# Key weights in two row pieces, five tiles only centred, two turned tiles copied by VectorE

## The chip, the cores and the metric

The kernel runs on one core of one Trainium2 chip. A core has TensorE (matrix products, in PSUM), VectorE, ScalarE, GpSimd and SyncE, which issues most of the DMAs; each works through its own queue of instructions in order, and they wait for each other through semaphores. In the profile they are PE (with PEld for its weight loads), DVE, ACT, POOL and SP. The metric is the device time of one execution in microseconds (us); the time of a kernel is the median of its runs.

## What is computed

One transformer block, forward and backward. The sequence has 2048 rows of 640, in bf16. The first half is linear attention with 32 heads of 20; the second a gated MLP of width 1728. The outputs are the block's output and the gradients of x and of the five weights.

```python
h  = x + A_ref(layernorm(x), wqkv, wo)
h2 = h + B_ref(layernorm(h), w1, w3, w2)

def A_ref(x, wqkv, wo):                        # per head
    q, k, v = split(x @ wqkv)
    phi = lambda t: where(t > 0, t + 1, exp(t)) + 1e-6
    pq, pk = phi(q), phi(k)
    kv  = einsum("bhsd,bhse->bhde", pk, v)
    z   = einsum("bhsd->bhd", pk)
    num = einsum("bhqd,bhde->bhqe", pq, kv)
    den = einsum("bhqd,bhd->bhq", pq, z) + 1e-6
    return (num / den) @ wo

out, vjp = jax.vjp(f, x, wqkv, wo, w1, w3, w2)
return out, *vjp(grad_out)
```

The layer norm subtracts each row's mean and divides by its standard deviation. Two facts about it matter here. A factor that belongs to a row can be applied after a product with that row instead of before. And `exp` and `relu` on ScalarE take such a factor (`scale`) at no extra instruction.

## The kernel before

The order of the work is written out by hand (a manual schedule): the program text fixes the order of every engine's queue, and pools of tiles with a fixed number of buffers fix what waits for what. The 2048 rows are 16 tiles of 128 rows, called tile 0 to tile 15 (t).

**Phase 1** is the loop over t near line 540, and takes the first 50 us. For each tile it needs the row statistics, the normalised rows turned so that the 640 columns lie on the partitions (`pqT`), the key features `pk_all`, and for some tiles the query features.

- *Statistics* (`Stats.part`, lines 145 to 155, `stat` in the step lists, "S"): two BN_STATS, an aggregate and an add on VectorE, then a power of -1/2 on GpSimd, which gives the factor `rs`.
- *Normalising* (`p1_norm`, line 247, "N", "A" and "L"): subtract the mean and multiply by `rs`, on VectorE; for the tiles 10, 12 and 14 on ScalarE (`on_act`), with a bias `nb` that GpSimd makes (line 170). In the step list "N" and "A"/"L" say when it is emitted: "N" before the tile's own features, "A" behind them, "L" last.
- *Turning*: tiles 0 to 7 on TensorE (`p1_tr`, line 253: five transposes into a PSUM tile `tr`, then one ScalarE copy to `pqT`, line 260); tiles 8 to 15 by a DMA transpose (line 251) that `p1_norm` issues on SP.
- *Key features*: `p1_mm` (line 274) multiplies two halves of 320 columns into a PSUM tile `big`, of which there are two; `phi` (line 290) takes `exp` and `relu` of it on ScalarE into `mq` and `rq` (three buffers each); a held closure `rest`, "R" in the step lists, does the minimum and the add on VectorE (lines 299, 300). The turn of tile t+1 stands between the two halves of tile t.
- *Query features*: in the steps 6, 7, 9 and 11, `q_tile` does the same with tiles 0 to 3. It uses the same two `big` tiles, the same `mq` and `rq`, and the same ScalarE queue.
- In the steps 3 to 6 `ghh_chunk` puts five matmuls of 512 columns of another product behind each tile. From step 7 on `m_part` (line 430) multiplies key features with the rows.

Tile 0 is only centred (`RAW = 1`): it is turned without its factor, `exp` and `relu` apply `rs`, and `p1_scale` (line 264, "C") multiplies the rows on VectorE in step 3, since `m_part` and the store of the normalised rows need them whole. Its key features come in two halves with four ScalarE instructions (line 535), each behind its own piece of the key weights.

`v_steps` lists, for each step t, what VectorE does and in which order.

**SP's queue at the start** is x row 0, x row 1, key weights columns 0 to 319, x row 2, key weights columns 320 to 639, x row 3, x rows 4 and 5, then transposed loads (`w2T`, `g2T`), x rows 6 to 9, `w2T`, the query weights in one piece, x rows 10 to 15. ("Row" stands for 128 rows.)

**Later places that the change touches.** Behind phase 1 the residual rows are loaded again (`load_x(0, 6)`), for the attention output (`f2_at`, lines 655 to 664), whose weights `Wp` come by five DMA transposes (line 709). Behind the second backward stage `q_parts` (line 1219) issues five DMA transposes `tri` (line 1226), read by the product `gkvT` (line 1388); SP also issues there the transposed normalised rows `load_xnT` (line 1242), the transposed query weights `load_wqT` (line 1299) and the key features `load_pk` (line 1410). The last loop (line 1335) computes 35 blocks of the gradients of w1 and w3; the first seven store each block in two halves.

Of the kernel before, what the change touches and what calls it, by code (L numbers as in the profile page):

```python
# [55 lines left out]
def kernel(  # L56
# [74 lines left out]
    class Stats:  # L131
# [10 lines left out]
                for j in range(2):  # L142
                    self.part(src, t, j)

        def part(self, src, t, j, mid=None):
            if j == 0:
                self.st[t] = cp.tile([P, 2, 6], F32, name="st6", bufs=4)
            V.bn_stats(out=self.st[t][:, j, :], in_=src[:, t, j * HD:(j + 1) * HD])
            if j == 0:
                return  # L150
            V.bn_aggr(out=self.mv[:, t, :], in_=self.st.pop(t)[:])
            if mid is not None:
                mid()
            V.tensor_scalar(out=self.ve[:, t:t + 1], in0=self.mv[:, t, 1:2], scalar1=EPS_LN, scalar2=None, op0=ALU.add)
            G.tensor_tensor(out=self.rs[:, t:t + 1], in0=self.ve[:, t:t + 1], in1=mhalf[:, 0:1], op=ALU.pow)
# [27 lines left out]
    def load_wq(a, b):  # L183
        dma(out=wqkv[:, :, a * HD:b * HD], in_=wq_v[:, :, a * HD:b * HD])

    def load_x(a, b):
        dma(out=x_sb[:, a:b, :], in_=xS[:, a:b, :])

    load_x(1, 2)
    A.activation(sg[:], zero[:], AF.Exp)  # L190
    load_wq(2, 3)
    load_x(2, 3)
    load_wq(3, 4)
    load_x(3, 4)
    load_x(4, 6)

    mask = cp.tile([P, DT, M_MAX], BF16, name="mask")

# [40 lines left out]

    XT_DMA = 8  # L240
    WARM = 34
    RAW = 1

    def on_act(t):
        return t > XT_DMA and t % 2 == 0
# [1 line left out]
    def p1_norm(t):  # L247
        xn = x_sb[:, t, :]
        (ln1.norm_act if on_act(t) else ln1.norm)(xn, xn, t)
        if t >= XT_DMA:  # L250
            dmaT(out=pqT[:, :, t * P:(t + 1) * P], in_=xn)

    def p1_tr(t, parts=((0, DT),)):
        xn = x_sb[:, t, :]
        for a, b in parts:
            tr = ps.tile([P, DT, P], BF16, name="tr", bufs=2)
            for c in range(a, b):
                T.transpose(tr[:, c, :], xn[:, c * P:(c + 1) * P], ident[:])

            A.copy(out=pqT[:, a:b, t * P:(t + 1) * P], in_=tr[:, a:b, :])  # L260

    def p1_scale(t):
        xn = x_sb[:, t, :]
        V.tensor_scalar(out=xn, in0=xn, scalar1=ln1.rs[:, t:t + 1], scalar2=None, op0=ALU.mult)

    def p1_half(acc, t, n0):
        for c in range(DT):
            T.matmul(acc, lhsT=pqT[:, c, t * P:(t + 1) * P], rhs=wqkv[:, c, n0:n0 + HD], start=(c == 0),  # L268
                     stop=(c == DT - 1))

    def p1_acc():
        return ps.tile([P, 2, 512], F32, name="big", bufs=2)

    def p1_mm(t, n0, between=None, halves=None):
        acc = p1_acc() if halves is None else None
        for j in range(2):
            p1_half(acc[:, j, 0:HD] if halves is None else halves[j][:, 0:HD], t, n0 + j * HD)
            if j == 0 and between is not None:
                between()
        return acc  # L280

    def two(ap):
        return ap.rearrange("p (j n) -> p j n", j=2)
# [3 lines left out]
    def phi_tiles():  # L287
        return [p1.tile([P, D], BF16, name=n, bufs=3) for n in ("mq", "rq")]

    def phi(acc, dst, t, parts=None):  # L290

        mq, rq = parts or phi_tiles()
        if parts is None:
            kw = dict(scale=ln1.rs[:, t:t + 1]) if t < RAW else {}
            A.activation(two(mq[:]), acc[:, :, 0:HD], AF.Exp, **kw)
            A.activation(two(rq[:]), acc[:, :, 0:HD], AF.Relu, **kw)

        def rest():
            V.tensor_scalar(out=mq[:], in0=mq[:], scalar1=1.0, scalar2=1e-6, op0=ALU.min, op1=ALU.add)
            V.tensor_tensor(out=dst, in0=mq[:], in1=rq[:], op=ALU.add)  # L300
        held.append(rest)
# [157 lines left out]
    zero_pads()  # L459
    load_w2T(0, 2 * P)  # L460
    load_g2T(0)
    load_x(6, 10)
    load_w2T(2 * P, 4 * P)
    load_wq(0, 2)
    load_x(10, ST)
    def warm_up(n, warm):
        for _ in range(n):
            T.matmul(warm[:, 0:P], lhsT=ones[:], rhs=ones[:], start=True, stop=True, skip_group_check=True)
# [12 lines left out]
    def stat(t):  # L481
        ln1.run(x_sb, t, t + 1)
        if on_act(t):
            ln1.bias(t)
# [1 line left out]
    ln1.part(x_sb, 0, 0)  # L486
    ln1.part(x_sb, 0, 1, center_first)
    p1_tr(0, ((0, 2), (2, DT)))
    warm_up(8, p1_acc()[:, 0])
    stat(1)  # L490
    p1_norm(1)
    ln1.part(x_sb, 2, 0)
    ln1.part(x_sb, 2, 1)
    ln1.part(x_sb, 3, 0)
    p1_norm(2)
    ln1.part(x_sb, 3, 1)
    ln1.part(x_sb, 4, 0)
    p1_norm(3)
    ln1.part(x_sb, 4, 1)
    w13 = [go for c0, c1 in ((0, 2), (2, 4), (4, 5)) for go in load_w13(c0, c1)]  # L500
    w13 += [lambda: dma(out=w1[:, :, F:FP], in_=rows(B_w3)[:, :, F - FL:F])]

    def load_wo():
# [2 lines left out]
    trickle = {4: w13[0], 5: lambda: w13[1](0, 1), 6: lambda: w13[1](1, 2), 12: w13[2]}  # L506

    R = None
    v_steps = {1: (R, ("N", 4)), 2: (("S", 5), R, ("N", 5)), 3: (("S", 6), R, ("N", 6), ("C", 0)),
               4: (("S", 7), R, ("N", 7), ("S", 8)), 5: (R, ("N", 8), ("S", 9)), 6: (R, ("N", 9), ("S", 10)),  # L510
               7: (("S", 11), R, R, ("A", 10), ("L", 11)), 8: (("S", 12), R, R, ("S", 13)),
               9: (("N", 13), R, ("S", 14), ("B", 12)), 10: (R, R, ("S", 15)), 11: (R, ("A", 14), ("L", 15))}
    V_OPS = {"S": stat, "N": p1_norm, "C": p1_scale}

    def xn_out(g, q):
        sl = slice(g * TPC, (g + 1) * TPC)
# [9 lines left out]
    M0 = {7: (0, 1, 2), 8: (3, 4, 5)}  # L526
    M0.update({t: (t - 3,) for t in range(9, ST)})
    for t in range(ST):
        first = None
        if t < RAW:  # L530
            first = phi_tiles()
            kh = [ps.tile([P, 512], F32, name="k0", tag="m", bufs=2) for _ in range(2)]

            def act(i, j):
                A.activation(first[i][:, j * HD:(j + 1) * HD], kh[j][:, 0:HD], (AF.Exp, AF.Relu)[i],
                             scale=ln1.rs[:, t:t + 1])

            def between():
                act(0, 0)
                p1_tr(t + 1)  # L540
                act(1, 0)
            k = p1_mm(t, D, between, kh)
            act(0, 1)
            act(1, 1)
        else:
            k = p1_mm(t, D, (lambda: p1_tr(t + 1)) if t + 1 < XT_DMA else None)
        steps = v_steps.get(t, (R,) * len(held))
        for step in steps:
            if step is R:
                held.pop(0)()  # L550
            elif step[0] in V_OPS:
                V_OPS[step[0]](step[1])
        phi(k, pk_all[:, t, :], t, first)
        for when in ("A", "B", "L"):
            for step in steps:
                if step is not R and step[0] == when:
                    p1_norm(step[1])
            if when == "A" and t in QT:
                q_tile(QT.index(t))
        if 3 <= t < 7:  # L560
            ghh_chunk(t - 3, lambda: ps.tile([P, 512], F32, name="gp", tag="m", bufs=2))
        m_part(0, M0.get(t, ()))
        if t >= 11:
            V.memset(bd[:, t - 11, :], 0.0)
            make_mask(t - 11)
        if t >= 9:
            m_part(1, [2 * (t - 9), 2 * (t - 9) + 1])
        for f, *n in outs.get(t, ()):
            f(*n)
        if t in trickle:  # L570
            trickle[t]()
# [66 lines left out]
        m_part(4, range(11, ST), (j,))  # L638
        m_end(4, (j,))
    ps.release()  # L640
    load_x(0, 6)


    ps = pool("pap", space=PSUM)
# [299 lines left out]
    def kv3():  # L944
# [2 lines left out]

    run((q_late, 10, f2_mT), (q_late, 11, kv3), (phi_rest,),
        (q_late, 12, lambda: (f2_wT(0), f2_wT(1))), (q_late, 13, lambda: (f2_wT(2), f2_wT(3))),
        (f2_wT, 4), (phi_rest,), (q_late, 14), (r_T, 4), (r_head, 5), (r_prod, 7),  # L950
        (q_out, 10, 14), (mlp_ghh, 4),
        (q_late, 15), (w2_room,), (sig_table,), (f2_half, 0, 0), (f2_half, 1, 0), (f2_half, 2, 0), (f2_half, 3, 0), (mlp_ghh, 5),
        (f2_half, 0, 1), (r_store, 4, 5), (f2_half, 1, 1), (f2_hn, 0), (r_store, 5, 6), (f2_half, 2, 1), (f2_hn, 1),
# [358 lines left out]
    load_xnT(1)  # L1312
    part(4)
    part(4)
    load_xnT(2)
    part(20)
    V.reduce_sum(out=gz[:], in_=gz8[:], axis=AX.X)


# [58 lines left out]
        for _ in range(n):  # L1378
            next(jobs, None)

    load_xnT(3)
    load_wqT(0)
    fill(4)
    for m, (a, b) in enumerate(M_H):
        n = (b - a) * DH
# [14 lines left out]
    small = bv.tile([P, ST, D], BF16, name="small", tag="hnN")  # L1400
    mN, gkv_b, gm = (small[:, n:n + DT] for n in (0, DT, 2 * DT))
    gzd = small[:, 3 * DT, :].rearrange("p (m q) -> p m q", q=P)
    dma(out=mN, in_=m_v)
    dma(out=rows(dwoT_d), in_=dwoT[:])

    dx = pool("dx", "right")

    def load_pk(c):
# [2 lines left out]

    gzb = dx.tile([P, D], F32, name="gzb")
    g_k = gqkv[1] = U1.tile([P, ST, D], BF16, name="g_k", tag="S0")
    for n in range(4):
        load_pk(n)

    for i, (c, ms) in enumerate(SQ_BLOCKS):
        unload(square(wqT[:, 2 * DT:, :], gkvT, i), gm[:, i, :])
# [136 lines left out]
    for i, (f0, f1) in enumerate(blocks):  # L1555
        n = f1 - f0
        for m in range(DT):
            last = (i, m) == (len(blocks) - 1, DT - 1)
            for a, b in ((0, n - P), (n - P, n)) if last else ((0, n),):
                c = (a + b) // 2  # L1560
                halves = ((a, c), (c, b)) if i * DT + m < 7 else ((a, b),)
                out = [(x + y - a, z + y - a, to) for y, w in halves for x, z, to in both_grads(m, f0 + y, f0 + w)]
                grad_job(hnN, m, lambda t: gb[i][:, t, a:b], b - a, out, A.dma_start)
        load_block(i + 2)
        if 0 < i <= 4:
            gw2_out(i - 1)
        if i < 4:
            gw2_turn(i)
# [36 lines left out]
```

## Time and profile before

| What | Value |
|---|---|
| median of 3 runs | 820.98 us (819.28 to 821.57) |
| the profiled execution | 820.36 us, its span 818.6 us |
| granted TensorE clock | 1.00 |
| PE busy | 811.6 us (99% of the span) |
| DVE, ACT, POOL busy | 452.7, 324.8, 131.7 us |
| DVE busy between 10 and 35 us | 22.36 of 25 us |
| ACT busy between 10 and 35 us | 22.52 of 25 us |
| first matmul of key features | 6.61 us from the span's start |
| from 700 us on | PE alone, DVE under 3 us in all |

The span goes from the first to the last instruction; 1.76 us of the profiled execution's time lie around it. The page gives the busy time of an engine with what each group of instructions cost, the time that it stood idle before them, and what ended that. Matmuls overlap, so PE's busy share hides waits shorter than a matmul; a wait is better seen in the timeline, from start to start. A line of the timeline is: start, duration, engine, line of the program, operation, written tile <- read tiles, shapes, how many were merged, and in brackets the idle time and what ended it. In a merged line the duration goes from the first start to the last end.

### The profile page before, as it was taken

The numbers are of one execution on the slowest core, as the hardware profiler recorded it, in microseconds if no ns is written. First come the engines' busy times: TensorE is split into PE (matmuls) and PEld (weight loads), VectorE is DVE, ScalarE is ACT, GpSimd is POOL, SyncE is SP. The second block draws the span as 40 slices with busy tenths as digits, with TensorE's granted clock in tenths as the row PEclk, the third lists the DMA queues.
The fourth block names the chain that finished last, engine by engine and source line by source line (L and its number), as shares of the span: only waits on it lengthen the run. The fifth ranks groups of instructions, "written<-read, shape, count | busy, mean of one in ns | idle before, by whom it ended". The sixth has DMA issues, their size and how long they took to land.

```text
span 818.6 us, 13711 instructions
## 1 busy us (share of the span) xinstructions
PE 811.6 (99%) x5261; PEld 501.6 (61%) x5292; DVE 452.7 (55%) x973; ACT 324.8 (40%) x609; POOL 131.7 (16%) x198
## 2 busy tenths in 40 slices
PE   9999999999999999999999999999999999999998
PEld 6777544555555555754577777777777777544444
DVE  7859997998898566300057777772781544200000
ACT  7856688665565666011112212222212334211111
POOL 2243333323222212100001111110220000000000
PEclk9999999999999999999999999999999999999999
DMA  9899899696485556999877877269994888979991
GB/s 262 207 242 277 206 276 302 207 244 174 128 209 158 169 168 168 239 254 243 233 178 181 218 194 193 58 111 181 269 217 93 179 193 153 249 175 235 221 239 37
DMA packets 335889, 162.46 MB, mean 198 GB/s; under 512 B 252560, under 2 KB 329072, under 8 KB 335824
## 3 DMA queue, kind: packets, MB, share of 16 engines
q1 hardware_dynamic: 291920, 120.68, 63.8%
q0 software_dynamic: 7328, 24.48, 8.9%
q10 hardware_dynamic: 36576, 16.42, 8.2%
q8 instruction: 41, 0.67, 0.3%
q14 instruction: 24, 0.20, 0.1%
HBM read 47.09 MB, written 53.43 MB: 123 GB/s over the span
## 4 chain that ended last, share of the span: by engine, by line
PE 96%; DMA 1%; ACT 1%; DVE 1%; issue 0%; SPq 0%; POOL 0%; DVEq 0%
PE mm L395 20%; PE job L1335 19%; PE ghn L1131 14%; PE gxn L1504 8%; PE gw L1086 7%; PE big L268 4%; PE o L913 4%; PE o L859 3%; PE gwo L1219 3%; PE macc L430 3%; PE gr L1188 3%; PE dkv L1441 3%; PE at L657 2%; DMA wqkv<-in_A_wqkv_dram 1%; PE dkv L1369 1%; DMA tri<-tri 1%
## 5 line engine op out<-in xcount | busy, mean ns | idle before, releaser
L1335 PE MATMUL job<-gb,hnN 128*128 128x496 bf16 (+3 forms) x576 | 116.8, 366 | 0.0
L1131 PEld LDWEIGHTS <-ggb 128*128 128x128 bf16 x864 | 84.5, 98 | 33.0
L395 PE MATMUL mm<-pqT,w 128*128 128x512 bf16 x396 | 93.2, 379 | 0.5
L1335 PEld LDWEIGHTS <-hnN 128*128 128x128 bf16 x576 | 55.8, 98 | 61.0
L395 PEld LDWEIGHTS <-w 128*128 128x128 bf16 x540 | 52.6, 98 | 62.9 <-issue 0.6
L1339 ACT CAST obs<-job 128x496 bf16<-128x496 f32 (+4 forms) x56 | 28.5, 510 | 123.6 <-PE job L1335 123.6
L1131 PE MATMUL ghn<-w13a,ggb 128*128 128x320 bf16 x448 | 63.5, 299 | 0.0
L1146 DVE SCALAR_TENSOR_TENSOR wb<-gs,hnb 128x640 f32<-128x640 bf16 x16 | 13.2, 825 | 88.1 <-ACT gs L1143 88.1
L1131 PE MATMUL ghn<-w13b,ggb 128*128 128x320 bf16 x416 | 61.4, 299 | 0.0
L395 PE MATMUL mm<-g2T,w2T 128*128 128x512 bf16 x228 | 58.8, 379 | 0.6
L1086 PE MATMUL gw<-hb,g 128*128 128x512 bf16 (+2 forms) x316 | 58.4, 345 | 0.2
L1086 PEld LDWEIGHTS <-g 128*128 128x128 bf16 x320 | 31.3, 98 | 27.0
L420 ACT CAST ghh<-mm 128x512 bf16<-128x512 f32 x48 | 28.2, 588 | 48.2 <-PE mm L395 41.4
L1196 POOL TENSOR_TENSOR sz<-Zb,g_h 128x640 f32<-128x640 bf16 x16 | 20.2, 1262 | 163.7 <-DVE g_h L1197 163.7
L796 ACT ACTIVATE sig<-mm 128x512 bf16<-128x512 f32 x56 | 33.7, 602 | 25.0 <-PE mm L395 21.6
L1143 ACT ACTIVATE gs<-ghn 128x640 bf16<-128x640 f32 x16 | 11.3, 705 | 76.0 <-PE ghn L1131 76.0
L395 PEld LDWEIGHTS <-w2T 128*128 128x128 bf16 x260 | 25.4, 98 | 23.4
L268 PEld LDWEIGHTS <-pqT 128*128 128x128 bf16 x320 | 30.7, 98 | 13.5 <-ACT pqT L260 0.9
L268 PE MATMUL big<-wqkv,pqT 128*128 128x320 bf16 x250 | 38.4, 299 | 0.2
L1335 PEld LDWEIGHTS <-g 128*128 128x128 bf16 x320 | 31.0, 98 | 11.5
L832 DVE TENSOR_TENSOR gate<-gate,sig 128x1024 bf16<-128x1024 bf16 x28 | 19.3, 689 | 33.9 <-ACT gate L807 31.1
L1091 ACT CAST gw2o<-gw 128x512 bf16<-128x512 f32 (+2 forms) x20 | 10.4, 519 | 66.6 <-PE gw L1086 25.3
(217 smaller groups left out, 1391.2 us busy)
## 6 DMA issues: line engine op xcount, KB each, us to landing
hh_d<-hhT SPq DMA_DIRECT2D x24, 256.0 KB, 2.8
gg_d<-gate POOLq DMA_DIRECT2D x24, 256.0 KB, 4.4
gg_d<-ghh POOLq DMA_DIRECT2D x24, 256.0 KB, 4.1
ggb<-gg_d SPq DMA_DIRECT2D x6, 896.0 KB, 5.3
ggb<-gg_d ACTq DMA_DIRECT2D x6, 832.0 KB, 5.7
ggb<-gg_d SPq DMA_DIRECT2D x2, 1728.0 KB, 13.9
pk_d<-pk_all SPq DMA_DIRECT2D x4, 640.0 KB, 5.4
g<-in_grad_out_dram SPq DMA_DIRECT2D x4, 640.0 KB, 5.7
```

The costliest lines, as they stand in the source:

```text
L268: T.matmul(acc, lhsT=pqT[:, c, t * P:(t + 1) * P], rhs=wqkv[:, c, n0:n0 + HD], start=(c == 0), stop=(c == DT - 1))
L395: T.matmul(acc[:], lhsT=w[:, c, fc * P:(fc + 1) * P], rhs=rhs[:, c, :], start=(c == 0), stop=(c == DT - 1))
L420: A.copy(out=ghh[n // 2][:, n % 2, :], in_=acc[:])
L430: T.matmul(macc[m][j][:, 0:n], lhsT=pk_all[:, t, m * P:(m + 1) * P], rhs=x_ext[:, t, j * HD:j * HD + n], start=(t == 0), stop=(t == ST - 1))
L796: A.activation(sig[:, i, :], gp[:], AF.Sigmoid)
L859: T.matmul(accs[i, j][:, 0:HD], lhsT=hhT[c][:, fc, i * P:(i + 1) * P], rhs=w2[:, fc, j * HD:(j + 1) * HD], start=(first and fc == 0), stop ...
L913: T.matmul(o2["ps"][:, 0:HD], lhsT=hhT[c][:, fc, i * P:(i + 1) * P], rhs=w2[:, fc, j * HD:(j + 1) * HD], start=(fc == 0), stop=(fc == FT - 1))
L1086: T.matmul(acc[:, 0:fw], lhsT=g2[:, t, m * P:(m + 1) * P], rhs=hb[b][:, t, 0:fw], start=(t == 0), stop=(t == ST - 1))
L1131: T.matmul(acc[:, j, 0:HD], lhsT=ggb[t // 2][:, k, lo:lo + P], rhs=rhs[:, j * HD:(j + 1) * HD], start=(k == 0), stop=(k == NG - 1))
L1335: T.matmul(acc[:, 0:n], lhsT=lhs[:, t, m * P:(m + 1) * P], rhs=rhs(t), start=(t == 0), stop=(t == ST - 1))
L1339: A.copy(out=ob, in_=acc[:, 0:n])
L1504: T.matmul(acc[:, j, 0:HD], lhsT=g, rhs=wqT[:, k, j * HD:(j + 1) * HD], start=(k == 0), stop=(k == 14))
```

## The change

- The key weights are loaded in two row pieces (`load_wk`: 2 of 5 blocks of 128 rows, then 3), all 640 columns. `first_mm` multiplies tile 0 block by block into both halves, with the turn of tile 1 behind the first two blocks. The four half-width ScalarE instructions of tile 0 become two of full width.
- `RAW = 5`: tiles 0 to 4 are only centred. `exp` and `relu` of their key features, and of the query features of tiles 0 to 3 and 4, take the factor. `p1_scale` multiplies the rows of the tiles 0 to 4 later, now on GpSimd: in step 3 tile 0, step 4 tile 1, step 5 tiles 2 and 3, step 6 tile 4.
- The turned tiles 2 and 3 are copied to `pqT` by VectorE instead of ScalarE. From step 3 on the turn of the next tile stands behind both halves of a tile, no longer between them.
- `v_steps` is written anew: "E" ends a tile's statistics and centres it, "P" is one half of BN_STATS. In step 7 both "R" come first, then N 9, S 10, S 11; before, N 9 and S 10 stood in step 6.
- x row 6 comes with rows 4 and 5; the query weights come in two pieces; 4 instead of 8 warm-up matmuls; the residual rows 4 and 5 are loaded apart, behind the transposes of the attention rows 4 and 5; `load_xnT(2)` behind all five `tri` transposes, `load_xnT(3)` and `load_wqT(0)` behind the `load_pk`; five instead of seven blocks of the last loop are stored in halves.

```diff
-        def part(self, src, t, j, mid=None):
+        def part(self, src, t, j, mid=None, end=True):
...
-            if j == 0:
-                return
+            if j and end:
+                self.end(t, mid)
+
+        def end(self, t, mid=None):
             V.bn_aggr(out=self.mv[:, t, :], in_=self.st.pop(t)[:])
...
+    def load_wk(a, b):
+        dma(out=wqkv[:, a:b, D:2 * D], in_=wq_v[:, a:b, D:2 * D])
+
     load_x(1, 2)
     A.activation(sg[:], zero[:], AF.Exp)
-    load_wq(2, 3)
+    load_wk(0, 2)
     load_x(2, 3)
-    load_wq(3, 4)
+    load_wk(2, DT)
     load_x(3, 4)
-    load_x(4, 6)
+    load_x(4, 7)
...
-    RAW = 1
+    RAW = 5
...
-            A.copy(out=pqT[:, a:b, t * P:(t + 1) * P], in_=tr[:, a:b, :])
+            copy(out=pqT[:, a:b, t * P:(t + 1) * P], in_=tr[:, a:b, :])
...
-        V.tensor_scalar(out=xn, in0=xn, scalar1=ln1.rs[:, t:t + 1], scalar2=None, op0=ALU.mult)
+        G.tensor_scalar(out=xn, in0=xn, scalar1=ln1.rs[:, t:t + 1], scalar2=None, op0=ALU.mult)
...
+    def first_mm(between):
+        acc = p1_acc()
+        for c in range(DT):
+            for j in range(2):
+                T.matmul(acc[:, j, 0:HD], lhsT=pqT[:, c, 0:P], rhs=wqkv[:, c, D + j * HD:D + (j + 1) * HD],
+                         start=(c == 0), stop=(c == DT - 1))
+            if c == 1:
+                between()
+        return acc
...
-    load_x(6, 10)
+    load_x(7, 10)
     load_w2T(2 * P, 4 * P)
-    load_wq(0, 2)
+    load_wq(0, 1)
+    load_wq(1, 2)
     load_x(10, ST)
...
-    warm_up(8, p1_acc()[:, 0])
-    stat(1)
-    p1_norm(1)
-    ln1.part(x_sb, 2, 0)
-    ln1.part(x_sb, 2, 1)
-    ln1.part(x_sb, 3, 0)
-    p1_norm(2)
-    ln1.part(x_sb, 3, 1)
-    ln1.part(x_sb, 4, 0)
-    p1_norm(3)
-    ln1.part(x_sb, 4, 1)
+    warm_up(4, p1_acc()[:, 0])
+    for t in (1, 2):
+        ln1.part(x_sb, t, 0)
+        ln1.part(x_sb, t, 1, lambda: center(t))
+    ln1.part(x_sb, 3, 0)
+    ln1.part(x_sb, 3, 1, end=False)
...
-    v_steps = {1: (R, ("N", 4)), 2: (("S", 5), R, ("N", 5)), 3: (("S", 6), R, ("N", 6), ("C", 0)),
-               4: (("S", 7), R, ("N", 7), ("S", 8)), 5: (R, ("N", 8), ("S", 9)), 6: (R, ("N", 9), ("S", 10)),
-               7: (("S", 11), R, R, ("A", 10), ("L", 11)), 8: (("S", 12), R, R, ("S", 13)),
-               9: (("N", 13), R, ("S", 14), ("B", 12)), 10: (R, R, ("S", 15)), 11: (R, ("A", 14), ("L", 15))}
+    v_steps = {1: (("E", 3), ("P", 4, 0)), 2: (("P", 4, 1), ("E", 4), R), 3: (("S", 5), R, ("N", 5), ("C", 0)),
+               4: (("S", 6), R, ("N", 6), ("C", 1)), 5: (("S", 7), R, ("N", 7), ("S", 8), ("C", 2), ("C", 3)),
+               6: (R, ("N", 8), ("S", 9), ("C", 4)), 7: (R, R, ("N", 9), ("S", 10), ("S", 11), ("A", 10), ("L", 11)),
+               8: (("S", 12), R, R, ("S", 13)), 9: (("N", 13), R, ("S", 14), ("B", 12)), 10: (R, R, ("S", 15)),
+               11: (R, R, ("A", 14), ("L", 15))}
...
+        turn = (lambda: p1_tr(t + 1, copy=V.tensor_copy if t in (1, 2) else A.copy)) if t + 1 < XT_DMA else None
+        k = p1_mm(t, D, turn, int(t > 2)) if t else first_mm(turn)
...
-    load_x(0, 6)
+    load_x(0, 4)
...
-        (f2_wT, 4), (phi_rest,), (q_late, 14), (r_T, 4), (r_head, 5), (r_prod, 7),
+        (f2_wT, 4), (phi_rest,), (q_late, 14), (r_T, 4), (r_head, 5), (load_x, 4, 6), (r_prod, 7),
...
     part(4)
     part(4)
+    part(20)
     load_xnT(2)
-    part(20)
...
-    load_xnT(3)
-    load_wqT(0)
     fill(4)
...
-    dma(out=mN, in_=m_v)
-    dma(out=rows(dwoT_d), in_=dwoT[:])
...
-    for n in range(4):
-        load_pk(n)
+    load_pk(0)
+    load_pk(1)
+    dma(out=mN, in_=m_v)
+    dma(out=rows(dwoT_d), in_=dwoT[:])
+    load_pk(2)
+    load_pk(3)
+    load_xnT(3)
+    load_wqT(0)
...
-                halves = ((a, c), (c, b)) if i * DT + m < 7 else ((a, b),)
+                halves = ((a, c), (c, b)) if i * DT + m < 5 else ((a, b),)
```

## The prediction

> **What bounds the kernel now.** I read the busy shares, then the chain that ended last, then PE's waits stretch by stretch, then the timeline of the first 35 us.
>
> ```profile
> PE 811.6 (99%) x5261; PEld 501.6 (61%) x5292; DVE 452.7 (55%) x973; ACT 324.8 (40%) x609; POOL 131.7 (16%) x198
> PE warm L468 <- DVE zero L125: 1.1, 1, 1.1
> PE k L268 <- DMA wqkv<-in_A_wqkv_dram: 0.6, 2, 0.4
> PE at L657 <- DVE rden L378: 0.2, 1, 0.2
> PE gkvT L1388 <- DMA tri<-tri: 0.5, 1, 0.5
> ```
>
> PE is the bound, and its chain share is 96%. What can be won is only where PE stands still: the key weights at 6 to 8 us, `at` near 85 us, `gkvT` near 566 us, and two waits of 0.27 us for ScalarE's copies of the turned tiles 2 and 3 (10.34 and 12.28 us). Start to start these are 0.93 (0.35 and 0.58), 0.41, 0.64 and 0.54 us: under 3 us in all. What can be lost lies between 10 and 35 us, where VectorE is busy for 22.36 of 25 us, and PE needs its rows.
>
> ```profile
> 14.56 0.32 DVE L299 TENSOR_SCALAR mq<-mq 128x640 bf16<-128x640 bf16 x1
> 14.98 0.49 DVE L300 TENSOR_TENSOR pk_all<-mq,rq 128x640 bf16<-128x640 bf16 x1
> 15.39 0.44 DVE L161 TENSOR_SCALAR x_sb<-x_sb,ln_mv,ln_rs 128x640 bf16<-128x640 bf16 x1
> 15.74 0.88 DVE L148 BATCH_NORM_STATS2 st<-x_sb 128x6 f32<-128x320 bf16 x2
> ...
> 28.03 0.92 ACT L166 ACTIVATE x_sb<-x_sb,nb,ln_rs 128x640 bf16<-128x640 bf16 x1
> 29.15 0.70 ACT L295 ACTIVATE mq<-big 128x640 bf16<-128x640 f32 x1 [0.20 <-DVE pk_all L300]
> 29.75 0.70 ACT L296 ACTIVATE rq<-big 128x640 bf16<-128x640 f32 x1
> 30.34 0.71 ACT L295 ACTIVATE mq<-big 128x640 bf16<-128x640 f32 x1
> 30.74 2.88 PE L268 MATMUL big<-wqkv,pqT 128*128 128x320 bf16 x20
> ```
>
> VectorE runs without a pause: from start to start an "R" (lines 299, 300) is 0.83 us, a norm 0.35, and a "S" with its aggregate 1.23 (13.33 to 14.56). The second part shows how little room PE has: the query features' `relu` ends at 30.45, and PE's next product into that `big` starts 0.29 us later.
>
> **The start, VectorE's order alone.** Tile 0's product now takes six matmuls behind the second weight piece instead of five (+0.13), which lands some 0.05 earlier by the bytes queued before it. VectorE's copies of the tiles 2 and 3 I price by the smaller VectorE copies out of PSUM, line 1422: 0.28 us for 256 columns and 0.35 for 384, so 0.48 for 640 by their slope, against 0.69 on ScalarE. PE is then 0.45 us ahead at tile 3. VectorE pays: two copies 0.96, and tile 4's statistics before the first "R". By the durations above: copy 2 to 10.51, centre 3 about 11.2, copy 3 to 12.20, tile 4 centred at 13.3, R to 14.15, S 5 to 15.4, R to 16.2, and N 5 starts at 16.2, where it started at 15.39: 0.8 late. From there to the end of S 10, before has 4 R, 4 N, 5 S and one "C" (0.38); after has 5 R and no C on VectorE: +0.83 - 0.38 = +0.45. S 10 is 1.3 us late (28.2 for 26.92).
>
> What waits for it: GpSimd makes `nb` 10, and ScalarE's norm of tile 10 goes from 28.03 to 29.3. Queued behind it stand `exp` and `relu` of query tile 1, with 0.20 us of idle time before them: they end 1.1 late, at 31.5 instead of 30.45. Less the 0.29 of room, PE is 0.8 late. VectorE then does S 11, the norm of 11 behind its power, and S 12 before the query tile 0's R, which ends near 32.5 instead of 29.9; that frees `mq`, and tile 8's `exp` and `relu`, which ended at 31.64, end at 33.9. PE's next product, due at 32.1, starts at 33.9: +1.8. At tile 11 and query tile 3 the same order costs once more, which I put at 0.6 (between 0 and the 0.83 of one R). Start without GpSimd: **+2.4 us** (bounds 0 and 3: if the 0.8 shrank under the room, nothing is late).
>
> **The five scalings on GpSimd.** No row has that operation. The nearest are GpSimd's two-input ones: 0.79 us for 320 columns (line 367), 1.26 for 640.
>
> ```profile
> L1196 POOL TENSOR_TENSOR sz<-Zb,g_h 128x640 f32<-128x640 bf16 x16 | 20.2, 1262 | 163.7 <-DVE g_h L1197 163.7
> ...
> 59.94 1.86 DVE L299 TENSOR_SCALAR mq<-mq 128x640 bf16<-128x640 bf16 x1
> 60.07 1.54 POOL L367 TENSOR_TENSOR pr<-hx,Zb 128x320 f32<-128x320 bf16 x2
> ```
>
> One input of 640 columns reads as many elements as two of 320, so I take 0.79 and keep 1.26 as the upper end. The last two lines matter more: VectorE's `tensor_scalar`, 0.32 us elsewhere, took 1.86 when GpSimd began 0.13 behind it, and ended 0.19 after GpSimd. So the operation isn't free to VectorE: a bf16 `tensor_scalar` (R's first half, N) meeting it waits for its end. Each C stands in GpSimd's queue right behind a power, so it starts when the N that waited for that power is due, or during the R before it. C 0 and C 1 hold N 5 and N 6 for all but about 0.2 us, C 2 and C 3 back to back N 8, C 4 an R: 5 x 0.79 - 4 x 0.2 = **+3.15 us** on a VectorE that never pauses (bounds 0, where they fall beside statistics, and 5.5 at 1.26). The powers of the tiles 6, 7, 9 and 10 also queue behind C's on GpSimd; VectorE needs them later than the C's end. BN_STATS rows beside a GpSimd operation aren't stretched, so the hold is only on these two forms.
>
> The Trainium skill ("GPSIMD Engine Reference", section 3.1) gives 1.03 cycles per element at 1.2 GHz for a bound one-input body, by which the operation would be an estimated 0.55 us and the sum 823.7. Its section 8 says that GpSimd shares SBUF interfaces with VectorE and contends with VectorE instructions that use two ports or two inputs; the 1.86 us above agrees.
>
> **Later.** `at` at 85 us: the fourth and fifth piece of work in the queue, a reload of x of 960 KB, landed at 83.44 ahead of `Wp`'s third transpose at 85.48; with 640 KB it lands some 0.8 earlier, so -0.4 (0 to -0.41). `gkvT`: its last `tri` was issued at 562.21, behind `load_xnT(2)`'s issue of 3.34 us from 558.77, though ScalarE had it ready at 561.45; it landed at 566.45. Ahead of that issue it goes 0.76 earlier: -0.6 (0 to -0.64; next late is nothing that the waits show).
>
> At nothing, with what hides it: the moved `load_xnT(3)`, `load_wqT(0)` and `load_pk` keep SP busy until about 616 instead of 608, and the last lands near 620, needed from 625 (4 us of room; if it is gone, the excess is paid whole); `load_xnT(2)` is read only from 604; the rows 4 and 5 of x land near 93, used at 95.06; x row 6 with 4 and 5 lands at 9.74 instead of 9.38, needed past 13; the query weights cost one SP issue of 0.58 more and are used from 22, landing near 21; the w13 load passes ahead of tile 8's transpose, which has 2.6 us of room (25.97 against 28.56); four warm-up matmuls fewer leave PE waiting for the same weights; two fewer blocks in halves are ScalarE DMA issues beside PE's last stage, and the last block is as before.
>
> Sum: 820.36 + 2.4 + 3.15 - 0.4 - 0.6 = **824.9 us**. The 820.36 is the profiled execution, 1.76 over its span of 818.6 and 0.62 under the median of 820.98, within the runs' spread.
>
> **The rivals.**
> *No hold by GpSimd* (C's fall beside BN_STATS, or the short one-input form doesn't keep VectorE off). For it: BN_STATS is over half of VectorE's time there. Against: the 1.86 us row, and that powers and N's come in pairs. Time: 820.36 + 2.4 - 1.0 = 821.8.
> *VectorE's lateness stays within PE's room* (other side). If statistics 3 starts earlier, or S 10's lateness of 1.3 comes out below the 0.20 us of ScalarE's idle time ahead of query tile 1 (the bracket above) and PE's 0.29, then PE keeps its 0.45 us lead of tile 3. It decides at 0.49 us of lateness of S 10. For it: the waits of 0.27 for the copies go. Against: 22.36 of 25 us busy. Time: 820.36 - 0.45 - 1.0 = 818.9, down to 818.4 with the second piece's waits halved.
> *The scaling is as long as the 1.26 row*: 820.36 + 2.4 + 5.5 - 1.0 = 827.3. For it: same width; against: one input and bf16 out.
>
> **How the numbers follow.** Hold by GpSimd at about 0.79: 0.63. Same at 1.26: 0.06. No hold: 0.15, of which 0.11 lies within 0.3% (2.46 us, about what a measurement of this kernel can tell from no change) and 0.04 above. Lateness within the room: 0.16, of which 0.10 under 818.52 and 0.06 not. Faster 0.10, same 0.17, slower 0.63 + 0.06 + 0.04 = 0.73. The range goes from 818.9 (the second rival's centre) to 827.3; it leaves out about 0.10 below and 0.05 above. The likeliest case's own range is 823.2 to 826.
>
> **What would show it.** Right: VectorE's line 161 or 299 rows of 0.8 to 1.2 us beside a GpSimd row of line 264; N 5 starting past 16; S 10 ending past 29; PE waiting on `big` for ScalarE between 28 and 36 us; PE's tile 8 to 11 products some 5 us late; no wait of 0.5 at `gkvT`. Wrong: line 264 rows on GpSimd beside unstretched VectorE rows; S 10 ending by 27.5; a new PE wait past 600 us for `pkT` or `xnT`, or at `at` (then the later gains turn into losses).

## The result, and the profile after

The changed kernel takes 826.82 us (median of 6 executions, 825.06 to 828.21) beside 820.40 us of the kernel before (6 executions): a ratio of 1.0081, with an interval of 1.0069 to 1.0093, so 5.7 to 7.6 us more. The forecast was 824.9 us, slower, with a range of 818.9 to 827.3. The profiled execution is the fastest of the six: 825.06 us, span 823.1, which is 4.5 us over the span before; some 2 us of the median's loss lie in executions that no trace here shows.

The busy shares of the page hardly move, and neither does PE's work:

```profile
PE 812.9 (99%) x5257; PEld 501.7 (61%) x5288; DVE 455.6 (55%) x974; ACT 324.1 (39%) x605; POOL 141.0 (17%) x203
```

GpSimd has 9.3 us more; the 1.3 us more of PE are, as will be seen, products at half the clock. What PE waited for, by the waits up to 40 us (the first three lines) and from 100 to 550 us (the last; columns: in total, times, longest):

```profile
PE gp L409 <- DMA g2T<-in_grad_out_dram: 2.0, 1, 2.0
...
PE big L273 <- ACT rq L310: 0.9, 1, 0.9
PE big L291 <- DMA wqkv<-in_A_wqkv_dram: 0.6, 1, 0.6
...
PE trh L764 <- DVE hn L163: 0.6, 1, 0.6
```

The waits of before at `at` and `gkvT` are gone. New is one of 2.0 us for the transposed gradient `g2T`, which the prediction doesn't name, one at `big` near 35 us for ScalarE, which it does, and one of 0.6 us near 100 us. PE's timeline around the first:

```profile
12.88 0.44 PE L263 MATMUL tr<-ident,x_sb 128*128 128x128 bf16 x5
15.28 0.47 PE L409 MATMUL gp<-g2T,w2T 128*128 128x512 bf16 x1 [1.96 <-DMA g2T<-in_grad_out_dram]
15.97 1.49 PE L409 MATMUL gp<-g2T,w2T 128*128 128x512 bf16 x3 [0.22 <-issue]
17.25 2.31 PE L273 MATMUL big<-wqkv,pqT 128*128 128x320 bf16 x10
```

Ten products took 2.31 us here and 1.52 elsewhere: the granted clock was 0.50 from 17 to 18 us. `g2T` landed at 15.24, against 12.78 before. The timelines of VectorE and of GpSimd show the copies and a norm beside a scaling:

```profile
9.18 0.49 DVE L265 COPY pqT<-tr 128x640 bf16<-128x640 bf16 x1 [0.59 <-PE tr L263]
...
10.96 0.49 DVE L265 COPY pqT<-tr 128x640 bf16<-128x640 bf16 x1 [0.25 <-PE tr L263]
...
15.39 0.92 DVE L163 TENSOR_SCALAR x_sb<-x_sb,ln_mv,ln_rs 128x640 bf16<-128x640 bf16 x1
16.23 0.87 DVE L148 BATCH_NORM_STATS2 st<-x_sb 128x6 f32<-128x320 bf16 x2
```

```profile
15.28 1.96 POOL L269 TENSOR_SCALAR x_sb<-x_sb,ln_rs 128x640 bf16<-128x640 bf16 x1
```

The norm of tile 5 took 0.92 us instead of 0.44, but it ended at 16.31, with GpSimd's operation (the second fence) at work until 17.24; and the statistics behind it were not stretched. The norm started at 15.39, as before, and not at the forecast 16.2. A copy by VectorE takes 0.49 us as estimated, but VectorE idles before it until PE has turned the tile.

The rest of the forecast chain, in ScalarE's timeline and in PE's:

```profile
31.19 0.92 ACT L168 ACTIVATE x_sb<-x_sb,nb,ln_rs 128x640 bf16<-128x640 bf16 x1 [0.78 <-POOL nb L172]
```

```profile
35.98 1.52 PE L273 MATMUL big<-wqkv,pqT 128*128 128x320 bf16 x10 [0.94 <-ACT rq L310]
```

ScalarE's norm of tile 10 comes 3.16 us later than before (28.03), and PE, which before doesn't wait at `big` at all, waits there.

To compare runs, I use one place: the six `macc` products that start at 39.16 us before. Their start, less 39.16, is called the lag; it holds everything that the start loses. It is 4.35 us in the profile of the changed kernel (43.52): 2.52 were lost by the first of these products (30.27 for 27.75), to `g2T` and the halved clock, and 1.83 behind it, where `big` is waited for. By the start of the same products, PE then is 4.52 us late ahead of `at` and 4.11 behind it (-0.41), 5.02 from `trh` on, 5.08 ahead of `gkvT` and 4.43 to the end (-0.65).

### The profile page after: what moved, and what is told of

Same layout as the page of the kernel before. It is cut to its first block, busy times and chain, and to the rows that moved or that the text cites. A ratio compares the mean times of both kernels' runs of the same rounds, so it can differ in the third digit from the quotient of the medians.

```text
span 823.1 us, 13716 instructions
## 1 busy us (share of the span) xinstructions
PE 812.9 (99%) x5257; PEld 501.7 (61%) x5288; DVE 455.6 (55%) x974; ACT 324.1 (39%) x605; POOL 141.0 (17%) x203
## 3 DMA queue, kind: packets, MB, share of 16 engines
q0 software_dynamic: 7328, 24.48, 8.8%
## 4 chain that ended last, share of the span: by engine, by line
PE 94%; DVE 4%; DMA 1%; issue 1%; ACT 0%; SPq 0%; POOL 0%; DVEq 0%; ACTq 0%
PE mm L409 20%; PE job L1331 19%; PE ghn L1127 14%; PE gxn L1501 8%; PE gw L1082 7%; PE o L909 4%; PE o L855 3%; PE gwo L1215 3%; PE gr L1184 3%; PE dkv L1438 3%; PE macc L444 2%; PE at L653 2%; PE big L273 2%; DVE st L148 1%; PE mm L273 1%; PE dkv L1365 1%
```

## The experiments

Theories at the outset. *Order*: VectorE's longer queue makes the statistics of tile 10 late, and with them ScalarE's norm and the features behind it; PE pays at `big`. *Hold*: GpSimd's scalings, which keep VectorE's `tensor_scalar` waiting, cause that lateness. *Landings*: late weights and the late `g2T` stop PE, and the clock falls. The ratios are to executions of the kernel before on the same chip.

| Run | Median, us | Ratio (95%) | Lag, us | Main PE waits up to 45 us |
|---|---|---|---|---|
| changed kernel | 826.82 | 1.0081 (1.0069 to 1.0093) | 4.35 | `g2T` 2.0, `big` 0.9 and 0.3 |
| e1 later edits undone | 827.52 | 1.0076 (1.0062 to 1.0090) | 5.48 | weights 1.4, `big` 2.8 |
| e2 before with the later edits | 820.33 | 1.0000 (0.9989 to 1.0010) | 0.22 | weights 1.2 in two |
| e3 scalings on VectorE | 826.80 | 1.0083 (1.0056 to 1.0109) | 6.38 | weights 2.0, `big` 2.0 and 0.2 |
| e4 no second warm-up | 827.35 | 1.0074 (1.0059 to 1.0089) | 7.31 | weights 1.9, `big` 2.8 |
| e5 old order | 829.42 | 1.0119 (1.0103 to 1.0134) | 7.63 | weights 1.5 in two, `big` 5.1 |
| e6 column pieces | 826.64 | 1.0105 (1.0068 to 1.0143) | 4.88 | weights 0.8 in two, `big` 4.0 in three |
| e7 order, columns, VectorE | 826.57 | 1.0085 (1.0068 to 1.0101) | 6.32 | weights 1.8 in two, `big` 3.5 |
| e8 fill between the pieces | 827.44 | 1.0094 (1.0081 to 1.0107) | 5.75 | `g2T` 0.7, `big` 2.8 and 0.4 |
| e9 copies on ScalarE | 825.96 | 1.0070 (1.0046 to 1.0094) | 3.51 | weights 1.4 in two, `big` 2.5 in three |
| e10 the same, scalings on VectorE | 824.41 | 1.0053 (1.0032 to 1.0073) | 2.05 | `big` 1.3 in two |
| e11 the same, R earlier | 826.91 | 1.0074 (1.0043 to 1.0105) | 0.74 | `big` 0.3 |
| e12 the same, column pieces | 822.07 | 1.0045 (1.0023 to 1.0068) | 0.72 | `big` 0.2 |

**e1 and e2: start and later edits apart.** e1 undoes all edits behind the start in the changed kernel; e2 makes these alone in the kernel before. The core of e2:

```diff
-    load_x(0, 6)
+    load_x(0, 4)
...
-    load_xnT(2)
     part(20)
+    load_xnT(2)
```

> The changed kernel with every edit behind the start undone (the reload of six x rows in one piece, the order of the transposed loads in the backward stage, seven blocks in halves). Theory A, the loss lies in the start and the later edits gain about 1 us at the products 'at' and 'gkvT': about 828, some 1.0 us over the changed kernel. Rival B, the later edits gain nothing in all, because the wait of 0.6 us at the transposes of hn near 100 us came with them: within 0.5 us of the changed kernel, 826 to 827.

> The kernel before with only the later edits. Theory A: 0.4 + 0.6 = 1.0 us faster than before, about 819.4. Rival B: the rows 4 and 5, loaded apart and later, make hn late and cost 0.6 us, so that 0.4 us remain: about 820. In its trace no wait of 0.5 at gkvT, none at 'at'.

The loss is in the start: e1 loses as much as the changed kernel, and e2 isn't slower. (e1's median, 827.52, lies between its two forecasts and doesn't decide between them.) In e2's trace the gains are there: `at` starts 0.18 us earlier than before, where PE was 0.22 late just ahead of it (-0.40), and what follows `gkvT` another 0.64. The times show none of it: between e2 and before the interval is 0.11% either way, 0.9 us, about the size of what was to be gained. The wait at `trh` isn't in e2, so the rows loaded later aren't enough to make it.

**e3: the scalings back on VectorE.**

```diff
-        G.tensor_scalar(out=xn, in0=xn, scalar1=ln1.rs[:, t:t + 1], ...
+        V.tensor_scalar(out=xn, in0=xn, scalar1=ln1.rs[:, t:t + 1], ...
```

> The changed kernel with the five scalings back on VectorE. If the hold by GpSimd sets the start's loss: VectorE's four norms of 0.92 us go back to 0.44 and the two stretched R to 0.32, 2.6 us less, and five scalings of 0.35 us come to it, 1.75: about 1 us faster than the changed kernel or more. If the late landing of the transposed gradient (15.24 for 12.78) with the slower clock behind it sets it: PE still stands still near 13.2 us for 2 us, and the time is within 1 us of the changed kernel.

The norms go back to 0.44 us, and yet no time is won. PE's timeline, and two rows of the windows (PE busy, PEld, DVE, ACT, POOL, then granted clock, DMA share, GB/s):

```profile
6.25 0.45 PE L263 MATMUL tr<-ident,x_sb 128*128 128x128 bf16 x5
8.66 1.76 PE L291 MATMUL big<-wqkv,pqT 128*128 128x320 bf16 x6 [1.96 <-DMA wqkv<-in_A_wqkv_dram]
10.21 1.54 PE L273 MATMUL big<-wqkv,pqT 128*128 128x320 bf16 x5
```

```profile
9.00:10.00 1.00, 1.00 (x6) 0.54 (x5) 0.89 (x2) 0.00 (x0) 0.00 (x0) 0.50 0.76 54
...
12.00:13.00 1.00, 1.00 (x10) 0.58 (x8) 0.79 (x3) 0.09 (x1) 0.00 (x0) 1.00 1.28 291
```

The second row piece landed at 8.62 us instead of 7.16 (15 of its 16 completions had come by 7.07); PE stood still for 1.96 us, ran at half the clock until past 11, and so turned tile 2 late. VectorE, whose copy stands ahead of all further statistics, idled for it:

```profile
9.06 0.89 DVE L148 BATCH_NORM_STATS2 st<-x_sb 128x6 f32<-128x320 bf16 x2 [1.28 <-DMA x_sb<-in_A_x_dram]
12.17 0.49 DVE L265 COPY pqT<-tr 128x640 bf16<-128x640 bf16 x1 [2.23 <-PE tr L263]
```

So another loss took the place of the hold in this execution. That is a new theory, *V*: VectorE's copies tie its whole queue to PE's progress.

**e4: does PE's instruction fetch make `g2T` late?** In the changed kernel's trace 15 of the 16 completions of `g2T` came from 13.55 to 13.76 us and the last at 15.24; a fetch of PE's instructions, 16 KB in one packet, began at 13.12 and took 1.08 us. e4 leaves out eight PE instructions ahead of it.

```diff
-    warm_up(4, p1_acc()[:, 0])
```

> The changed kernel without the four warm-up matmuls behind the turn of tile 0, that is eight PE instructions fewer ahead of the first product gp. Theory F, PE's instruction fetch of 16 KB (13.12 us, 1.08 us long) held the last of the 16 semaphores of the transposed gradient, 15 of which had come by 13.76: the fetch now falls behind gp, the load lands at 13.8, PE stands still 0.6 us instead of 2.1 and keeps its clock, and the time falls by 1 to 2 us, until VectorE's hold binds. Rival G, the transposes themselves are late by the order of the loads: the landing stays near 15.2 and the time stays.

`g2T` landed at 13.81 with all 16 completions together, and the fetch came at 17.11. The time didn't fall (827.35). The landing fits, but PE was also 1.9 us late for its weights, and in e1 a fetch at 12.76 held up nothing (`g2T` at 13.35). The fetch is not shown to be the cause. One other profile has such a landing, e8: 15 completions by 13.47, the last at 14.96, a fetch at 12.73, and a wait of 0.7 us.

**e5: the old order of the steps 6 and 7.**

```diff
-  6: (R, ("N", 8), ("S", 9), ("C", 4)), 7: (R, R, ("N", 9), ("S", 10), ("S", 11), ("A", 10), ("L", 11)),
+  6: (R, ("N", 8), ("S", 9), ("C", 4), ("N", 9), ("S", 10)), 7: (("S", 11), R, R, ("A", 10), ("L", 11)),
```

> The changed kernel with N 9 and S 10 back in step 6 (behind C 4) and S 11 ahead of both R in step 7. Theory O, the lateness of S 10 and so of nb 10, ScalarE's norm of tile 10 and the features queued behind it makes PE wait for 'big' near 32 us (2.0 to 2.8 us in three runs, with a halved clock for some 3 us behind it): R 5 and R 6 come behind S 10 again, so it ends 0.8 us earlier, and query tile 0's R no longer stands behind S 12; the wait falls to under 1 us, the clock stays, and the time falls by 2.5 to 4 us, to about 823.5. Rival H, GpSimd's hold on VectorE makes the lateness: a wait of over 2 us stays and the time falls by under 1 us.

A miss: slower, and the wait at `big` grew to 5.1 us. VectorE's and ScalarE's timelines tell why:

```profile
28.87 0.92 DVE L163 TENSOR_SCALAR x_sb<-x_sb,ln_mv,ln_rs 128x640 bf16<-128x640 bf16 x1 [2.12 <-POOL ln_rs L157]
```

```profile
33.17 0.70 ACT L309 ACTIVATE mq<-big 128x640 bf16<-128x640 f32 x1 [5.96 <-DVE pk_all L314]
```

The norm of tile 9 now stands ahead of both R; its power waits in GpSimd's queue behind C 2 and C 3 (24.48 to 28.30 in this run), and ScalarE can't write tile 7's `exp` because the R that frees `mq` is behind all that. So the new order of these steps isn't what loses: with the old one both R come later still (32.16 and 32.99 here, 25.66 and 26.89 in the changed kernel).

**e6: key weights in column pieces, tile 0 half by half.**

```diff
-    load_wk(0, 2)
+    load_wq(2, 3)
...
-    load_wk(2, DT)
+    load_wq(3, 4)
...
-        k = p1_mm(t, D, turn, int(t > 2)) if t else first_mm(turn)
+        k = p1_mm(t, D, turn, int(t > 2))
```

> The changed kernel with the key weights in two column pieces as before and tile 0 multiplied half by half. Theory P, the row pieces make one wait of 1.4 to 2.0 us near 7 to 8.6 us, and at 2.0 the clock halves for some 2.5 us: without them two waits of about 0.3 and 0.6 us come back, the clock stays at 1.00 until 30 us, and PE is 1 to 3 us earlier at gp; but what is gained is lost again at 'big' near 32 us, if VectorE's order sets that stage (theory O): time within 1.5 us of the changed kernel. Rival, the start up to 9 us decides: 2 to 3 us faster, 824.

Here PE has no long standstill early and is level with the kernel before up to 24 us (0.00 at `gp`), so the chain of the prediction is seen alone. ScalarE's timeline, then PE's:

```profile
31.72 0.92 ACT L168 ACTIVATE x_sb<-x_sb,nb,ln_rs 128x640 bf16<-128x640 bf16 x1 [2.82 <-POOL nb L172]
32.55 0.78 ACT L309 ACTIVATE mq<-big,ln_rs 128x640 bf16<-128x640 f32 x1
33.23 0.78 ACT L310 ACTIVATE rq<-big,ln_rs 128x640 bf16<-128x640 f32 x1
35.15 0.70 ACT L309 ACTIVATE mq<-big 128x640 bf16<-128x640 f32 x1 [1.15 <-DVE hx L314]
```

```profile
34.06 1.52 PE L273 MATMUL big<-wqkv,pqT 128*128 128x320 bf16 x10 [2.77 <-ACT rq L310]
36.50 1.52 PE L273 MATMUL big<-wqkv,pqT 128*128 128x320 bf16 x10 [0.93 <-ACT rq L310]
```

The norm of tile 10 starts 3.7 us later than before (28.03), and PE waits for the features behind it, then for those that wait for query tile 0's R (`hx`). The lag goes from 0.2 to 4.88 in this stretch alone, with the clock at 1.00. What PE had won or lost before matters little to it: at the first `macc` e6, e8 and e1 are 0.21, 0.67 and 0.70 us late and the changed kernel 2.52, and they end the start at 4.88, 5.75, 5.48 and 4.35.

**e7: order, columns and VectorE's scalings together.** The edits of e3, e5 and e6.

> Old order of steps 6 and 7, column pieces, and the scalings on VectorE, all else as in the changed kernel. If order, pieces and hold are all that loses: the two waits for ScalarE's copies (0.54 us) and 0.8 us of the later edits are gained, and 5 x 0.35 us more on VectorE costs up to 1.2 us: 819.5 to 821. If one more part loses (the turns behind both halves, the centred tiles), it stays over 822.

A miss as well: ScalarE waits 4.09 us for the R ahead of tile 7's `exp`, PE 3.5 at `big`. As in e5, the old order puts both R behind the statistics of tile 11. Of the start's larger edits e7 also keeps the copies by VectorE, the centred tiles and the place of the turns.

**e8: PE kept busy between the two row pieces.**

```diff
             if c == 1:
                 between()
+                warm_up(FILL, ps.tile([P, 512], F32, name="warm", tag="m", bufs=2))
...
+    FILL = 26
```

> The changed kernel with 26 warm-up matmuls (1.4 us at the full clock) between tile 0's first four products and the second weight piece, where PE stood still for up to 2.0 us. If the halved clock from 9 to 11.5 us comes of that standstill, it stays at 1.00 there and PE's lag at gp is 1 us or more lower than in the runs with a 1.9 us wait; the time falls by 0 to 1 us, because the wait at 'big' takes it back (theory O). Rival, the clock halves by something else (the DMA load, the product's shape): it stays 0.50 at 9 to 11 us.

PE's timeline, and the clock in the windows:

```profile
6.52 1.61 PE L485 MATMUL warm<-ones 128*128 128x128 bf16 x26
8.20 0.97 PE L292 MATMUL big<-wqkv,pqT 128*128 128x320 bf16 x6
```

```profile
9.00:10.00 1.00, 1.00 (x13) 0.80 (x11) 0.48 (x2) 0.73 (x2) 0.00 (x0) 1.00 0.82 135
```

The six products took 0.97 us instead of 1.76, and the clock stayed. But the second weight piece landed at 8.16 us here, not at 8.62. In e1 it landed at 8.18, and there the clock stayed without any filling: PE stood still for 1.44 us, and the six products took 0.97 too. So neither their shape nor the load of the DMA engines (a share of 0.82 here, 0.76 in e3) halves the clock, but that the filling kept it up isn't shown. At the second `gp` PE is 0.55 us late in e8 and 0.52 in e1, beside 1.95 in e3; e8 and e1 both lose at `big` (2.8 us) what they had kept.

**e9 and e10: the copies on ScalarE, with the scalings on GpSimd and on VectorE.**

```diff
-        turn = (lambda: p1_tr(t + 1, copy=V.tensor_copy if t in (1, 2) else A.copy)) if t + 1 < XT_DMA else None
+        turn = (lambda: p1_tr(t + 1)) if t + 1 < XT_DMA else None
```

> The changed kernel with the turned tiles 2 and 3 copied by ScalarE, as before. Theory V: VectorE's copies stand in its queue ahead of the statistics of the tiles 3 to 9, so VectorE waits for PE's turns, and so for the second weight piece (0.6 + 0.25 us idle in the changed kernel's profile, up to 2.2 us in two others), and works 0.98 us longer: what PE waits for, VectorE's whole queue now loses too, and it comes back at 'big' near 32 us. Without the copies VectorE is 1.8 to 3 us earlier at N 5, the wait at 'big' falls from 2 to 2.8 us to under 1 us, PE waits 0.3 us for each of the two copies, and the time is 2 to 4 us lower, 823 to 825. Rival O2, the order of the steps 3 to 7 and GpSimd's scalings are enough: the wait at 'big' stays over 1.5 us, the time within 1.5 us of the changed kernel.

> The same with the scalings on VectorE too, so that neither the wait for PE nor GpSimd's hold is there. If the hold costs what VectorE's rows show (four norms 0.48 us longer, two R 0.67 together, 2.6 us), less 1.75 us for the five scalings on VectorE: 0.5 to 1 us faster than the run with GpSimd's scalings. If GpSimd's hold costs nothing at the end: the same time within 0.5 us, or slower by up to 1.

Without the copies VectorE doesn't wait for PE at all in this stretch, N 5 starts at 14.55 (15.39 in the changed kernel, 16.41 in e1), and the lag is 3.51. But the waits at `big` stayed at 2.5 us, and the median fell by only 0.86: for e9 alone the rival's forecast (O2) holds, not theory V's. With the scalings on VectorE too the lag is 2.05. With the copies on ScalarE the hold thus costs 1.46 us at the lag and 1.55 in the medians; with them on VectorE (the changed kernel to e3) removing it gained nothing. What the copies cost depends in the same way on the rest: 0.84 us at the lag and 0.86 in the medians beside GpSimd's scalings (the changed kernel to e9), 4.3 and 2.4 beside VectorE's (e3 to e10; much of the 4.3 is e3's late weights, to which the copies tie VectorE). Each lag is one execution's, and the intervals of each of these pairs overlap. Even those of the changed kernel and of e10, without copies and hold, do so by a little (1.0069 to 1.0093 and 1.0032 to 1.0073).

e9's profiled execution is no faster than the changed kernel's (825.39 and 825.06 us), since its product `kv` at 75 us waited 1.6 us for a transposed tile `mT`. Waits of 0.8 to 1.6 us stand there in e4 and e7 to e11 and not in the other profiles; why wasn't tried.

**e11 and e12: the R earlier, with row pieces and with column pieces.** On top of e10:

```diff
-  ... 7: (R, R, ("N", 9), ("S", 10), ("S", 11), ("A", 10), ("L", 11)),
-  8: (("S", 12), R, R, ("S", 13)), 9: (("N", 13), R, ("S", 14), ("B", 12)), ...
+  ... 7: (R, ("N", 9), ("S", 10), ("S", 11), R, ("A", 10), ("L", 11)),
+  8: (R, ("S", 12), R, ("S", 13)), 9: (R, ("N", 13), ("S", 14), ("B", 12)), ...
```

> Copies on ScalarE and scalings on VectorE, and R moved in the steps 7 to 9: the second R of step 7 behind S 11, one R of step 8 ahead of S 12, the R of step 9 ahead of N 13. Theory Q, what is left of the start's loss in the run before it (2.05 us at 41 us, waits at 'big' of 1.0 and 0.3) is that query tile 0's R stands behind S 12 and that VectorE idles 0.67 us for GpSimd's power of tile 11 and of tile 13: the lag at 41 us falls to 0.3 to 0.9 us, the time by 1 to 1.7, to about 823. Rival, VectorE's work in all (one R more in these steps) sets it: the lag stays at 1.7 to 2.1 and the time within 0.5 us.

> The same with the key weights in column pieces, on a base where VectorE no longer takes back what PE gains early. If the row pieces cost something of their own (one wait of 1 to 2 us instead of two of 0.35 and 0.58): 0.3 to 1 us faster than the run with row pieces. If they cost nothing: the same within 0.5 us.

The lag falls to 0.74 and 0.72 as theory Q has it: the late place of the R was 1.3 us of the start's loss. Row pieces and column pieces come out alike at the lag.

In the time it can't be seen in e11, whose executions lie anywhere from 820.69 to 830.63. Its profile has another loss near 608 us, as e10's does. PE's and VectorE's timelines in e10:

```profile
615.63 2.83 PE L1438 MATMUL dkv<-small,xnT 128*128 128x320 bf16 x10 [4.64 <-DVE gp L1441]
```

```profile
613.82 0.83 DVE L1442 SCALAR_TENSOR_TENSOR g_k<-pkb,gp 128x640 bf16<-128x640 bf16 x1 [5.02 <-DMA pkb<-pk_d]
```

A piece of the key features, issued by GpSimd at 596.43, landed 17.3 us later; beside it SP took 10.6 us to issue one transposed load of query weights, 4.5 to 5 us in e12 and the changed kernel. With the halved clock behind it, PE is 7.0 us later from there on, and 6.4 in e11, whose lag just ahead of it was 0.79. e1, whose loads stand in the old order, has a milder form of it: 6.1 us for that issue, a piece landing 13.3 us after its own, and a PE wait of 0.7. So e12 and e11 can't be compared by their times, and the row pieces' own price stays open beyond the lag.

No version beats the kernel before: the best with the start's edits is e12, 2.5 us over it. In e12's profile the start isn't what is left. PE is 0.78 us late up to 84 us and 2.05 from 96 us on: `at` waits 1.3 us there for transposes of `Wp`, as it does for 0.7 to 1.4 us in e1, e3, e4 and e8 and not in the changed kernel. Why wasn't tried.

## Why the prediction was right, and where it was wrong

**Slower by some 4 to 6 us, from VectorE's queue, paid at `big`: right.** The chain, `nb` 10, ScalarE's norm of tile 10, query tile 1, query tile 0's R, `mq`, was there in every run with VectorE's long queue (e1, e3, e6, e8, e9: waits at `big` of 2.2 to 4.0 us in all), and moving the R cut it (e10 to e11). The prediction put the start at 5.55 us, 2.4 for the order and 3.15 for the hold; e6 shows 4.88 for both. By the lags it has three parts: the order with all else of the start 2.05 (e10), the hold 1.46 (e9 less e10), and what is left to e6, 1.4, which I put down to the copies; but e6 and e9 differ in the pieces too, so this last part is argued. In the profiled execution of the changed kernel more than half of the 4.35 us came another way, by `g2T` and the clock, which the prediction doesn't have. That the sum fits this execution is luck; that it fits the kernel is less so, as e6, e8 and e1 lose as much with only 0.2 to 0.7 us gone ahead of the chain.

**"The operation isn't free to VectorE: a bf16 `tensor_scalar` meeting it waits for its end": the first half right, the second wrong.** GpSimd's operation took 1.94 us (median of five), not 0.79, and was mis-sized by 2.5 times; VectorE's norm was held only 0.48 us each time, not until the end. Four norms and two R make 2.6 us where 3.15 was forecast: two errors that nearly cancel. Going by 1.94 and "waits for its end", the hold would have been put at 8.9 us. By the Trainium skill ("GPSIMD Engine Reference", section 3.1) the operation would be an estimated 0.55 us. No row here comes near; all five ran beside VectorE, so the operation alone isn't shown. The Trainium skill's rule on the shared interfaces (the same page, section 8) names VectorE instructions that use two ports or two inputs. The trace agrees in that norms were held and statistics were not; but R's add, with two inputs, was not held beside a scaling either (0.49 us at 26.48, as elsewhere).

**"Two copies 0.96": the price right (0.49 each), the wait left out.** The prediction priced the copies as work, and placed them by PE's turns of the profile before; it has no term for what VectorE loses when a turn comes late. In the changed kernel PE turned tile 2 early (8.70 for 9.50), so that N 5 came 0.8 us ahead of its forecast although VectorE had idled 0.84 us for PE; in e3, with late weights, it idled 2.5 us and N 5 started at 18.32. This is the step that failed, a wait added to VectorE with the statistics of five tiles and more behind it.

**"Tile 0's product ... (+0.13)": wrong in kind.** It reckoned the landing from the bytes ahead of it. The second row piece lands anywhere between 7.16 and 8.62 us in these runs, and PE waits for it in one stretch of 0.56 to 1.96 us in the changed kernel, e1, e3 and e4. Where that came to 1.92 and 1.96 (e4, e3), the clock fell to 0.50 for 3.4 us. The Trainium skill ("TensorE: Matmul & The Clock Gate", Part 1) has the clock fall after at least one idle window of about 3.4 us that runs free of the kernel. The traces agree on the length and on the free run: the clock changes only at multiples of 3.41 us, counted from another point in each run (halved from 8.42 to 11.83 in e3, from 15.44 to 18.85 in the changed kernel). They don't agree that all of the window is idle: PE was busy for 1.66 us (e3) and 1.45 (the changed kernel) of the 3.41 ahead of the fall. e6's standstill of 2.77 us at `big` fell on two such windows, with 1.65 and 1.52 us of work, and left the clock at 1.00; where the limit lies these figures don't show. In the end this, too, was in part taken back at `big`: e3 is 1.4 us behind e1 and e8 at the second `gp`, and 0.6 to 0.9 at the lag.

**The later gains: right in the trace (-0.41 of 0.4, -0.65 of 0.6), not seen in the time.** e2 has them in its trace and not in its median, and in e3 and e12 the later edits don't keep `at` from waiting 1.4 and 1.3 us for `Wp`. `trh` took 0.6 to 0.9 us of it back in the changed kernel, without a cause that was tried.

**What was costed at nothing.** `load_xnT(3)`, `load_wqT(0)` and `load_pk` are hidden in the changed kernel's profile and in e2, as said. In e10 and e11 they are not: a wait of 4.6 us and a loss of 6.4 to 7.0 stand there. The milder form in e1 says that the moved loads aren't its only cause; whether they make it worse stays open, as no run moved them alone on that base. Nor does the prediction price the factor on ScalarE: with it an `exp` or `relu` of 640 columns takes 0.80 us on average, without it 0.71, and 18 of them up to 45 us have it in the changed kernel. What that costs PE no run shows.

**The rivals.** *No hold*: refuted by the rows. Where the hold is really gone, its term for the order, 2.4, is near e10's lag of 2.05, but e10's time (824.41) is not near its 821.8. *Lateness within PE's room*: its place was right, S 10; with the copies on ScalarE and the R earlier (e11, e12) the lateness does shrink to that (`nb` 10 at 28.07 and 28.04 for 27.73). *The 1.26 us row*: nearer in time (827.3) by an operation even longer than 1.26, though the hold was shorter than it says.

## What to carry to other kernels

Before an engine with a full queue takes over a copy, ask what the copy waits for: the wait is then that of everything behind it, and it can be more than the work (2.5 us beside 0.98 for two copies in e3). Where several stages lose to the same queue, mending an early one (pieces, clock, order) can give nothing while a later one still loses: five runs here (e3, e4, e6, e7, e8) moved waits and not the time, and only removing copies, scalings and late R together brought the lag from 4.35 to 0.7 us. Even then (e12) the time stayed 2.5 us over, and the profile shows the next wait, at `at`. A gain of under 1 us at a wait that the trace names is real in the trace and may still be lost to the spread of the landings.

## What the runs showed of the hardware beyond that

- A bf16 scaling of 128 x 640 on GpSimd took 1.88 to 1.96 us beside VectorE (0.38 on VectorE), and held a VectorE `tensor_scalar` for 0.48 us, BN_STATS not at all.
- PE's granted clock fell to 0.50 after standstills of 1.96 us (e3, and `g2T` in the changed kernel), for 3.41 us each, and stayed at 1.00 after one of 1.44 (e1) and one of 2.77 (e6).
- The same load in the same place of the queue landed up to 1.5 us apart from run to run (the second row piece at 7.16 to 8.62 us).
- A load's last completion came 1.5 us after the 15 others (`g2T` at 15.24 in the changed kernel and 14.96 in e8, the second row piece at 8.62 in e3), and copies on GpSimd's queue landed 17 us after issue beside transposed loads on SP's.
